# Decay attention, gated MLP and a top-1 mixture of experts on one core: the decay's bias by a matmul, swapped keys from the transpose

## The chip, the cores and the metric

The kernel runs on one NeuronCore of a Trainium2 chip. A core has a matrix engine (PE, with weight loads as PEld), a vector engine (DVE), a scalar engine (ACT), a general engine (POOL), and a queue engine (SP) that here issues nearly all transfers; 16 DMA engines move the data. Each engine runs its instructions in the order in which they were written to it. The metric is the device time of one execution in microseconds (us).

## The reference

Inputs: q, k, v of shape (4 batches, 8 heads, 576 positions, 64), forget gates f of shape (4, 8, 576), and the weights of two MLPs; output: 2304 x 512 in float32.

```python
scores = scale * np.matmul(q, k.transpose(0, 1, 3, 2))
log_f = np.log(np.clip(f, 0.0001, 1.0))
cum = np.cumsum(log_f, axis=-1)
decay = cum[:, :, :, None] - cum[:, :, None, :]
scores = np.where(causal, -1000000000.0, scores + decay)   # causal: key after query
...                                                        # softmax over keys
attn_out = np.matmul(attn, v)
x = attn_out as (2304, 512)
x = (silu(x @ w_gate) * (x @ w_val)) @ w_out               # d_ff 1536
...                                                        # x to one of 8 experts, 512 -> 1024 -> 512
```

In a softmax over keys the term cum[query] cancels, so only -cum[key] has to enter a row of scores. It is the same for all 576 query rows of a head.

## The kernel before

**Stages.** The program works on 32 heads, two heads (a pair P) at a time, 16 pairs, four pairs a batch. One head is two items: query blocks 0 to 2 (64, 128 and 128 rows; g = 0) and blocks 3 and 4 (128 rows each; g = 1), so 64 items. `slot(i)` (line 439) issues three things: `part1(i)`, the scores, row maxima and exponentials of item i; `part2(i-1)`, the split of the exponentials in two f16 parts and their DMA transpose; `pv(i-2)`, the product with the values. In the same slots the next pair is prepared: `scales`, `prep_v`, `prep(P+1, 0)`, `prep(P+1, 1)` and the loads of the pairs after it. The first 18 slots (batch 0) run while the gated MLP's weights, stored as 8-byte numbers, are loaded and decoded (`decode`, line 836). Then MLP units (`unit`, line 1067; 9 groups of 256 tokens with 6 units each, a unit being 24 + 24 matmuls of line 490 and 12 of line 543) are written between the remaining slots by a pacing table (`pts_`, line 1117): batch 1's slots within units 5 to 10, batch 2's within 11 to 23, batch 3's within 24 to 34. The units left and the experts follow without attention.

**Precision.** q and k are scaled by a power of two and split into f16 high and low parts; a head's `qks` tile holds, per 128-position chunk, 64 columns high and 64 columns low. One DMA transpose (line 210) turns it into `qkt` with dimensions on the partitions: high on 0 to 63, low on 64 to 127. A score is high x high + low x low (line 244, q and k with equal halves) plus high x low + low x high (line 246), for which the key's halves are swapped: `ksw`, made by two DVE copies (lines 214, 215) that wait for the transpose.

**The bias.** The cumulative sums `fz` (32 heads x 576) go to the DRAM tensor `cum_d` (line 757). For each head one row is loaded into all 128 partitions (`cb`, line 218, on SP), multiplied by the pair's scale on POOL (line 219), and subtracted by DVE's `tensor_tensor_reduce` (line 310), which also takes the row maximum. For batches 0 to 2 (`inner`) the causal mask is a third matmul (line 250); for batch 3 it is added to `cb` on POOL in place (line 290), and line 310 then runs in two pieces, one against `cb` and one against the masked tile.

**Order.** The program is not run as written line by line: a scheduler places each engine's instructions by its own estimate of when they could start, so an edit can also shift instructions that it doesn't name. Buffers are rings: two each of `qks` and `qkt`, five score tiles `s`, four of `p16`, three PSUM banks for scores.

**Other names.** `jk` (line 185) is scratch in the `qks` ring; `mx`, `nb`: row maxima and the bias of the exponential; `pt`: transposed probabilities; `xr`: attention output, transposed, the MLP's input; `raw`, `wg`, `wv`: raw weight buffers; `vr`: values read once more for a batch's scale; `id_d`, `g_d`: routing tables in DRAM, written once per 256 tokens, four bytes at a time.

## Time and profile before

| | |
|---|---|
| median of 3 runs | 1080.13 us (1072.58 to 1081.8) |
| profiled execution | 1090.63 us, its span 1088.5 us |
| mean granted TensorE clock | 0.917 of full |
| busy share of the span | PE 81%, DVE 62%, ACT 49%, POOL 42% |
| DMA | 149.55 MB, 259697 of 298584 packets under 512 B |
| scores start / end | 19.9 us / 609 us |

The profile gives, for one execution, each instruction's start and duration, and for idle time of an engine what ended it. Busy shares over the whole span mix stages with different limits, so they are read by stage: batch 0 with the weight loads, 0 to 175 us; MLP units alone, 175 to 225; batch 1 with its units, 225 to 295; batch 2, 295 to 470; batch 3, 470 to 612; MLP and experts without attention, from 612. A PE duration holds the whole latency of a matmul; back to back matmuls overlap, so their price is the distance between starts.

### The profile page before, as it was taken

Reading aid. Unit: us, or ns where it says so; the run is one execution under the profiler, and the core shown is the slowest. Engines: PE = TensorE matmul, PEld = TensorE weight load, DVE = VectorE, ACT = ScalarE, POOL = GpSimd, SP = SyncE. Lnnn points to the kernel's source line nnn. Section 1 sums busy time; section 2 is a strip of 40 time slices with the busy share of each in tenths; the row PEclk is TensorE's granted clock in tenths of the full one; section 3 lists DMA queues with packets and bytes.
Section 4 is the critical chain, followed back from the end, with each engine's and each line's share of the span. In section 5 each row is a group of like instructions: output and inputs, shape, how many; then the busy total and the mean of one; then the engine's idle time right before and its main releaser. Section 6 shows DMA issues by size and latency. Waiting matters only on the chain. (4 is left out here: it accounts for less than half of the span.)

```text
span 1088.5 us, 19531 instructions
## 1 busy us (share of the span) xinstructions
PE 880.6 (81%) x6789; PEld 726.5 (67%) x6789; DVE 677.0 (62%) x1946; ACT 537.0 (49%) x1160; POOL 458.3 (42%) x544
## 2 busy tenths in 40 slices
PE   1444448887976859899788899999877998999995
PEld 1333337765855648677667678888767887898994
DVE  4899799586675757777587542233334776665450
ACT  5877778464555636546264332222213645554441
POOL 2487676555344634466477412222215732110111
PEclk9995558998987979999989999999988999999998
DMA  8899889257778897767567360102328996555420
GB/s 222 186 228 221 189 171 216 63 121 158 166 102 155 144 127 155 148 108 147 84 103 155 45 194 11 40 1 39 59 48 207 255 218 190 167 181 164 173 100 31
DMA packets 298584, 149.55 MB, mean 137 GB/s; under 512 B 259697, under 2 KB 272113, under 8 KB 298484
## 3 DMA queue, kind: packets, MB, share of 16 engines
q1 hardware_dynamic: 294144, 137.83, 57.7%
q0 software_dynamic: 4096, 10.24, 3.9%
q8 instruction: 54, 0.88, 0.4%
q14 instruction: 46, 0.38, 0.2%
q10 hardware_dynamic: 244, 0.22, 0.1%
HBM read 91.06 MB, written 10.38 MB: 93 GB/s over the span
## 5 line engine op out<-in xcount | busy, mean ns | idle before, releaser
L490 PE MATMUL g<-xr,wg 128*128 128x256 f16 x1296 | 166.4, 282 | 18.9 <-ACT xr L433 10.5
L490 PE MATMUL v<-xr,wv 128*128 128x256 f16 x1296 | 170.1, 283 | 1.8 <-DVE t L523 1.2
L490 PEld LDWEIGHTS <-wv 128*128 128x128 f16 x1296 | 129.6, 103 | 32.9 <-issue 11.4
L490 PEld LDWEIGHTS <-wg 128*128 128x128 f16 x1296 | 125.1, 101 | 38.3 <-issue 16.9
L345 POOL TENSOR_TENSOR p<-st,p 128x128 f16<-128x128 f32 (+3 forms) x128 | 111.9, 880 | 45.1 <-DVE p L342 34.8
L530 POOL TENSOR_TENSOR lo<-t,hi 128x512 fp32r<-128x512 f32 x54 | 71.1, 1316 | 138.4 <-ACT hi L529 123.3
L380 PE MATMUL px<-vs,pt 128*128 128x64 f16 x1280 | 62.8, 207 | 65.1 <-DMA pt<-p 56.8
L380 PEld LDWEIGHTS <-pt 128*128 128x128 f16 x1280 | 55.6, 108 | 80.8 <-DMA pt<-p 64.2
L320 ACT ACTIVATE st<-st,nb,c 128x64 f32<-128x64 f32 (+4 forms) x160 | 102.7, 643 | 2.0
L342 DVE CAST p<-st 128x64 f16<-128x64 f32 (+4 forms) x160 | 74.4, 484 | 19.7 <-ACT st L320 16.2
L356 POOL TENSOR_TENSOR p<-st,p 128x64 f16<-128x64 f32 (+1 forms) x128 | 57.0, 448 | 54.0 <-issue 34.7
L529 ACT ACTIVATE hi<-t 128x512 fp32r<-128x512 f32 x54 | 33.7, 624 | 85.1 <-DVE t L523 85.1
L977 POOL DMA_INDIRECT out_dram<-o,ix x24 | 25.4, 1057 | 114.9 <-ACT o L1216 71.4
L244 PE MATMUL ps<-qkt 128*128 128x64 f16 (+3 forms) x192 | 54.6, 316 | 20.7 <-DVE mx L310 14.6
L1214 PE MATMUL bank<-whi,h 128*128 128x512 f32 x200 | 66.8, 399 | 3.7 <-ACT h L1176 2.9
L513 ACT ACTIVATE t<-g,gscale 128x512 f32<-128x512 f32 (+3 forms) x72 | 39.3, 570 | 60.2 <-PE g L490 60.1
L516 DVE SCALAR_TENSOR_TENSOR t<-t,g 128x512 f32<-128x512 f32 x54 | 36.8, 681 | 47.2 <-ACT t L513 45.4
L943 DVE TENSOR_TENSOR wlo<-wr,whi 128x1024 fp32r<-128x1024 f32 x48 | 57.6, 1244 | 13.7 <-ACT whi L942 12.9
L219 POOL TENSOR_TENSOR cb<-cb,c 128x576 f32<-128x576 f32 x32 | 38.5, 1204 | 61.2 <-DMA cb<-cum_d 53.5
L543 PE MATMUL yp<-wohi,hi 128*128 128x512 f32 x144 | 60.0, 417 | 0.0
L1171 PE MATMUL bank<-xh,whi 128*128 128x320 f32 (+1 forms) x192 | 59.4, 312 | 0.5 <-ACT xh L93 0.5
L246 PE MATMUL ps<-ksw,qkt 128*128 128x64 f16 (+2 forms) x192 | 56.5, 318 | 4.0 <-DVE ksw L215 3.9
(295 smaller groups left out, 2295.1 us busy)
## 6 DMA issues: line engine op xcount, KB each, us to landing
wr<-in_moe_w_dram SPq DMA_DIRECT2D x72, 512.0 KB, 5.0
cb<-cum_d SPq DMA_DIRECT2D x32, 288.0 KB, 4.3
vr<-in_v_dram SPq DMA_DIRECT2D x16, 288.0 KB, 4.9
qk_in<-in_q_dram SPq DMA_DIRECT2D x32, 128.0 KB, 2.7
qk_in<-in_k_dram SPq DMA_DIRECT2D x32, 128.0 KB, 3.0
v_in<-in_v_dram SPq DMA_DIRECT2D x32, 128.0 KB, 3.8
y_d<-ys SPq DMA_DIRECT2D x6, 512.0 KB, 3.4
wg<-in_moe_w_gate_dram SPq DMA_DIRECT2D x5, 512.0 KB, 4.4
```

Of the source, the lines that this page charges most:

```text
L246: pe.matmul(out=ps[:, o:o + n], lhsT=lq, rhs=ksw[:, k0 - 64:k1 - 64], start=False, stop=(d1 <= d0), skip_group_check=True)
L320: act.activation(out=sts[m], in_=sts[m], func=ACTF.Exp, scale=c[:, 0:1], bias=nb[:, m:m + 1], accum_out=sm[:, m, hh:hh + 1],)
L342: vec.tensor_copy(out=flat[:, o + 64:o + 64 + n], in_=src)
L345: gp.tensor_tensor(out=flat[:, o1:o1 + n - 64], in0=src[:, 64:n], in1=flat[:, o + 128:o + 64 + n], op=ALU.subtract)
L356: gp.tensor_tensor(out=blk[:, :, 0:64], in0=pair, in1=blk[:, :, 64:128], op=ALU.subtract)
L380: pe.matmul(out=px[:, 128 * m + 64 * hh:128 * m + 64 * hh + 64], lhsT=pm[:, o + ph * last + c, :], rhs=vs[:, hh, c, vh, :], start=(c == 0 ...
L490: pe.matmul(out=ps[:, fi, :], lhsT=w16[:, j, kk, wi, 128 * fi:128 * fi + 128], rhs=xr[:, kk, x0:x0 + 2, xi, :], start=(n_ == 0), stop=(n_ ...
L530: last["lo"] = gp.tensor_tensor(out=lo, in0=t, in1=hi.bitcast(F32), op=ALU.subtract)
L543: pe.matmul(out=yps[g][i], lhsT=hx[:, fi, 128 * i:128 * i + 128], rhs=wo[fk][wx], start=(j == 0 and n_ == 0), stop=(j == KF // 2 - 1 and n ...
L943: (eng or vec).tensor_tensor(out=l_, in0=t, in1=h_.bitcast(F32), op=ALU.subtract)
L1171: pe.matmul(out=p, lhsT=w[wi][:, kk, 128 * fk:128 * fk + 128], rhs=x[xi][:, kk, c0:CAP], start=(n_ == 0), stop=(n_ == 3 * KD - 1),)
L1214: pe.matmul(out=p[0:m, :], lhsT=hx, rhs=wx, start=(n_ == 0), stop=(n_ == len(prods) - 1))
```

## The change

`cum_d` and `cb` go. The cumulative sums are split once into three bf16 pieces that together hold them, and kept in SBUF as `cum3`: partitions 32 i to 32 i + 31 hold piece i of all 32 heads. A one-time table `pick` is -1 where the partition's head equals the column's head; per pair ACT scales it into `nc`, 128 columns for each head. A matmul with `nc` as weights and `cum3` as moving operand then adds -scale x cum[key] to every row of a score tile. The DVE step stays and subtracts a zero. The mask is a matmul for all four batches (`MB`, `inner`, `masked` and POOL's additions go). `qks` grows from 10 to 15 chunks of 128 columns: the second copy of the keys has its halves swapped, its high half written by the same ACT instruction as the first (output of 640 instead of 320 elements), its low half by one more ACT copy. The DMA transpose delivers the swapped keys in `qkt[:, 2]`, and the two DVE copies go.

```diff
@@ consts @@
+        pick_i = c_p.tile([128, B * H], I32, tag="c", name="pick_i")
+        gp.iota(pick_i, [[-1, B * H]], base=0, channel_multiplier=1)
+        vec.tensor_single_scalar(out=pick_i, in_=pick_i, scalar=B * H - 1, op=ALU.bitwise_and)
+        vec.tensor_scalar(out=pick, in0=pick_i, scalar1=0.0, scalar2=-1.0, op0=ALU.is_equal, op1=ALU.mult)
+        vec.memset(cum3, 0.0)
+        vec.memset(zero, 0.0)
@@ scales @@
+        nc_ = st_p.tile([128, 2, 128], BF16, tag="nc", bufs=2, name="nc")
+        h0 = P // NP * H + 2 * (P % NP)
+        act.activation(
+            out=nc_, in_=pick[:, h0:h0 + 2].rearrange("p (h o) -> p h o", o=1).to_broadcast([128, 2, 128]),
+            func=ACTF.Copy, scale=c[:, 1:2],
+        )
@@ prep @@
-        qks = qks_p.tile([128, 2, NCH, 2, D], F16, tag="qks", name="qks")
-        for a in range(2):
+        qks = qks_p.tile([128, 3 * NCH, 2, D], F16, tag="qks", name="qks")
...
+        for a, n in ((0, 1), (1, 2)):
...
-            act.activation(out=hi, in_=src, func=ACTF.Copy, scale=s1)
+            act.activation(
+                out=part(w, w + D, 2) if n > 1 else hi, func=ACTF.Copy, scale=s1,
+                in_=src.rearrange("p (o c) d -> p o c d", o=1).to_broadcast([128, 2, NCH, D]) if n > 1 else src,
+            )
             vec.scalar_tensor_tensor(out=lo, in0=src, scalar=s1, in1=hi, op0=ALU.mult, op1=ALU.subtract)
...
-        ksw = qkt_p.tile([128, S], F16, tag="ksw", name="ksw")
-        vec.tensor_copy(out=ksw[0:64, :], in_=qkt[64:128, 1, 64:])
-        vec.tensor_copy(out=ksw[64:128, :], in_=qkt[0:64, 1, 64:])
-        cb = cb_p.tile([128, S], F32, tag="cb", name="cb")
-        b, h = P // NP, 2 * (P % NP) + hh
-        sp.dma_start(out=cb, in_=cum_d[b * H + h:b * H + h + 1, :].to_broadcast([128, S]))
-        gp.tensor_tensor(out=cb, in0=cb, in1=c[:, 1:2].to_broadcast([128, S]), op=ALU.mult)
-        heads[P, hh] = (qkt, ksw, cb)
+        act.activation(out=qks[:, 2 * NCH:, 0, :], in_=lo, func=ACTF.Copy)
+        qkt = qkt_p.tile([128, 3, NCH * 128], F16, tag="qkt", name="qkt")
+        sp.dma_start_transpose(out=qkt.rearrange("p a (c t) -> p (a c) t", t=128), in_=flat)
+        heads[P, hh] = (qkt, c[1][:, hh, :])
@@ score @@
-        d0, d1 = max(k0, 128 * j), k1 if inner else max(k0, 128 * j)
+        pe.matmul(out=ps[:, o:o + n], lhsT=lq, rhs=qkt[:, 2, k0:k1], start=False, stop=False, skip_group_check=True)
+        d0 = max(k0, 128 * j)
         pe.matmul(
-            out=ps[:, o:o + n], lhsT=lq, rhs=ksw[:, k0 - 64:k1 - 64], start=False, stop=(d1 <= d0), skip_group_check=True
+            out=ps[:, o:o + n], lhsT=pk, rhs=cum3[:, k0 - 64:k1 - 64], start=False, stop=(k1 <= d0),
+            skip_group_check=True,
         )
@@ part1 @@
-        if not inner:
-            for m in range(nt):
...
-                gp.tensor_tensor(
-                    out=sts[m][:, k0 - 64:k1 - 64], in0=cb[:, k0 - 64:k1 - 64], in1=masked[:, k0 - k1 + 128:], op=ALU.add
-                )
...
-                d0 = k1 if inner else min(max(k0, 128 * j), k1)
-                for a, b, bias in ((k0, d0, cb), (d0, k1, sts[m])):
...
+                vec.tensor_tensor_reduce(
+                    out=sts[m][:, k0 - 64:k1 - 64], in0=ps[:, o:o + n], in1=zero.to_broadcast([128, n]),
+                    scale=1.0, scalar=init, op0=ALU.subtract, op1=ALU.max, accum_out=mx[:, x:x + 1],
+                )
@@ start @@
-        act.dma_start(out=cum_d, in_=fz)
+        for i in range(3):
+            hi = c_p.tile([128, S], BF16, tag="c", name="cumhi")[0:B * H]
+            vec.tensor_copy(out=hi, in_=fz)
+            vec.tensor_copy(out=cum3[B * H * i:B * H * i + B * H, :], in_=fz)
+            if i < 2:
+                vec.tensor_tensor(out=fz, in0=fz, in1=hi, op=ALU.subtract)
```

The scheduler moves more than these lines. On SP, at the start of the program, before the change (`wg_91`: a raw weight buffer; `vr`: the values of batch 0; `qkt<-qks`: head 0's transpose):

```order
L826 DMA raw<-in_moe_w_gate_dram 128x4x256
L826 DMA wg_91<-in_moe_w_gate_dram 128x4x256
L794 DMA vr<-in_v_dram 128x576 x4
L210 DMA_TRANSPOSE qkt<-qks 128x10x128
L218 DMA cb<-cum_d 128x576
```

and with the change:

```order
L832 DMA raw<-in_moe_w_gate_dram 128x4x256
L832 DMA wg_92<-in_moe_w_gate_dram 128x4x256
L800 DMA vr<-in_v_dram 128x576 x4
L832 DMA wv_93<-in_moe_w_val_dram 128x4x256
L832 DMA wg_92<-in_moe_w_val_dram 128x4x256
L832 DMA wv_93<-in_moe_w_out_dram 128x1024
L170 DMA qk_in_98<-in_k_dram 128x4x64
L170 DMA qk_in_99<-in_q_dram 128x4x64
L168 DMA qk_in_98<-in_k_dram 64x2x64
L170 DMA qk_in_98<-in_k_dram 128x4x64
L168 DMA qk_in_99<-in_q_dram 64x2x64
L231 DMA_TRANSPOSE qkt<-qks 128x15x128 x2
```

Three weight loads of 512 KB and five pieces of the next pairs' q and k now stand ahead of the first two heads' transposes, which are issued together. On DVE, where the first 256 tokens are routed in the midst of batch 1 (`rb`, `eq`: routing; `t`, `xs`: MLP and attention output; lines 310 and 311 are the reduction on scores), before:

```order
L689 TENSOR_TENSOR rb<-eq,tokm 128x2x24
L713 TENSOR_TENSOR rb<-eq,gw 128x2x24
L214 COPY ksw<-qkt 64x576
L215 COPY ksw<-qkt 64x576
L342 CAST p_0_101<-st 128x448
L310 ISA st,mx<-ps,cb 128x64
L310 ISA mx 128x1
L310 ISA st,mx<-ps,cb 128x192
```

and with the change:

```order
L690 TENSOR_TENSOR rb<-eq,tokm 128x2x24
L714 TENSOR_TENSOR rb<-eq,gw 128x2x24
L517 SCALAR_TENSOR_TENSOR t<-t,g 128x512
L807 TENSOR_SCALAR gscale<-sw,sv 128x6
L410 TENSOR_TENSOR xs<-xn,xs 128x3x128
L808 SCALAR_TENSOR_TENSOR hscale<-sw,sv,gscale 128x6
L311 ISA st,mx<-ps,zero,mx 128x512
L311 ISA mx 128x1
L717 TENSOR_TENSOR ixf<-ixf,rk 128x48
L311 ISA st,mx<-ps,zero 128x64
```

Behind the routing steps stood the two copies that wait for a transpose, with the casts and reductions of other items behind them; now nothing on DVE at this place waits for a transpose of keys.

## Rows read from the trace of the kernel before

**Rows 1.** Busy time by stage: us, busy (xinstructions) per engine, granted clock, DMA share, GB/s.
```profile
0.00:175.00 175.00, 74.08 (x588) 52.92 (x589) 145.33 (x406) 129.22 (x312) 111.77 (x124) 0.78 0.90 205
225.00:295.00 70.00, 59.85 (x568) 47.86 (x568) 51.45 (x144) 41.14 (x105) 36.93 (x48) 0.93 0.71 147
295.00:470.00 175.00, 140.83 (x1356) 112.67 (x1355) 120.72 (x432) 90.84 (x240) 81.61 (x109) 0.88 0.82 139
470.00:612.00 142.00, 124.49 (x1183) 99.28 (x1181) 106.06 (x396) 68.87 (x177) 85.54 (x132) 0.96 0.64 114
```

**Rows 2.** PE's waits, 225 to 612 us: us in total, times, longest.
```profile
PE px L380 <- DMA pt<-p: 35.4, 18, 11.0
PE ps L244 <- DVE mx L310: 11.0, 8, 4.6
```

**Rows 3.** Waits of DVE and POOL, 225 to 612 us.
```profile
DVE ksw L214 <- DMA qkt<-qks: 37.7, 10, 9.8
...
POOL cb L219 <- DMA cb<-cum_d: 39.8, 11, 6.8
```

**Rows 4.** Timeline of DVE: start, us, instruction, [idle before <-releaser].
```profile
309.30 0.30 DVE L214 COPY ksw<-qkt 64x576 f16<-64x576 f16 x1 [6.58 <-DMA qkt<-qks]
...
402.21 1.46 DVE L214 COPY ksw<-qkt 64x576 f16<-64x576 f16 x1 [9.76 <-DMA qkt<-qks]
...
545.26 0.30 DVE L214 COPY ksw<-qkt 64x576 f16<-64x576 f16 x1 [6.55 <-DMA qkt<-qks]
```

**Rows 5.** Timeline of PE, its stops near these places.
```profile
226.00 0.19 PE L246 MATMUL ps<-ksw,qkt 128*128 128x64 f16 x1 [2.21 <-DVE ksw L215]
...
310.92 0.56 PE L770 MATMUL tot<-am,onesf 128*128 128x2 f32 x2 [6.01 <-DVE mx L310]
...
401.29 0.55 PE L380 MATMUL px<-vs,pt 128*128 128x64 f16 x7 [11.03 <-DMA pt<-p]
...
480.55 4.45 PE L490 MATMUL g<-xr,wg 128*128 128x256 f16 x24 [2.43 <-DVE t L516]
...
546.26 0.61 PE L244 MATMUL ps<-qkt 128*128 128x512 f16 x1 [4.62 <-DVE mx L310]
```

**Rows 6.** The clock after such a stop: columns as in rows 1.
```profile
314.00:316.00 2.00, 2.00 (x7) 1.61 (x6) 1.97 (x6) 0.51 (x3) 1.97 (x5) 0.50 0.10 17
```

**Rows 7.** Chain of waits, late MLP: start, us, 24 matmuls of one unit.
```profile
689.41 2.64 PE g L490 x24
```

**Rows 8.** Groups of instructions, 0 to 620 us: busy, mean ns, idle before.
```profile
L214 DVE COPY ksw<-qkt 64x576 f16<-64x576 f16 x32 | 18.5, 580 | 44.7 <-DMA qkt<-qks 44.1
...
L215 DVE COPY ksw<-qkt 64x576 f16<-64x576 f16 x32 | 12.7, 396 | 0.5
...
L219 POOL TENSOR_TENSOR cb<-cb,c 128x576 f32<-128x576 f32 x32 | 38.5, 1204 | 61.2 <-DMA cb<-cum_d 53.5 <-PE ps L246 4.5 <-DVE ys L574 2.5
...
L310 DVE CUSTOM_DVE_ANT_0 st<-ps,cb 128x64 f32<-128x64 f32 x56 | 12.1, 216 | 4.8 <-POOL cb L219 3.9 <-PE ps L250 0.7
...
L290 POOL TENSOR_TENSOR st<-cb,masked 128x128 f32<-128x128 f32 x32 | 14.3, 472 | 0.0
```

**Rows 9.** Timeline of PE: score matmuls back to back; distances of starts.
```profile
494.08 0.35 PE L244 MATMUL ps<-qkt 128*128 128x448 f16 x1
494.27 0.35 PE L246 MATMUL ps<-ksw,qkt 128*128 128x448 f16 x1
494.46 0.19 PE L244 MATMUL ps<-qkt 128*128 128x64 f16 x1
```

**Rows 10.** ACT groups that price the new ACT work.
```profile
L207 ACT ACTIVATE qks<-qk_in,sc 128x320 f16<-128x320 f32 x64 | 30.8, 549 | 8.4 <-DVE sc L780 8.4
...
L185 ACT ACTIVATE jk<-qk_in 128x640 f16<-128x640 f32 x32 | 23.3, 729 | 39.6 <-DMA qk_in<-in_k_dram 21.9 <-DMA qkt<-qks 15.6 <-DVE fz L756 1.8
```

**Rows 11.** Two us each: one lone 8-chunk transpose (262 KB); plain weight loads.
```profile
706.00:708.00 2.00, 2.00 (x21) 1.79 (x19) 0.00 (x0) 0.00 (x0) 1.19 (x1) 1.00 0.71 131
632.00:634.00 2.00, 2.00 (x21) 1.80 (x19) 0.69 (x1) 0.69 (x1) 0.00 (x0) 1.00 0.94 354
```

More of the change, by code (lines that the diff above doesn't have):

```diff
@@ L21 @@
 MASKED = -float(2 ** 100)
-MB = 3
 EXP1 = 1 << 23
@@ L84 @@
     rg = const.tile([128, KD, 32], F32, name="rg")
+    cum3 = const.tile([128, S], BF16, name="cum3")
+    pick = const.tile([128, B * H], F32, name="pick")
+    zero = const.tile([128, 1], F32, name="zero")
     sel = const.tile([128, NE], F32, name="sel")
@@ L201, in prep, with part @@
         sc, c = stt[P]
-        qks = qks_p.tile([128, 2, NCH, 2, D], F16, tag="qks", name="qks")
-        for a in range(2):
+        qks = qks_p.tile([128, 3 * NCH, 2, D], F16, tag="qks", name="qks")
+        flat = qks.rearrange("p c h d -> p (c h d)")
+        w = 2 * NCH * D
+        def part(o, step, n):
+            dims = [list(flat.ap[0])] + ([[step, n]] if n > 1 else []) + [[2 * D, NCH], [1, D]]
+            return type(flat)(flat.tensor, flat.offset + o, dims)
+        for a, n in ((0, 1), (1, 2)):
             src = qk_in[(2 * P + a) % NQK][:, hh]
             s1 = sc[:, 0, a:a + 1]
-            hi, lo = qks[:, a, :, 0, :], qks[:, a, :, 1, :]
-            act.activation(out=hi, in_=src, func=ACTF.Copy, scale=s1)
-            vec.scalar_tensor_tensor(out=lo, in0=src, scalar=s1, in1=hi, op0=ALU.mult, op1=ALU.subtract)
-        qkt = qkt_p.tile([128, 2, NCH * 128], F16, tag="qkt", name="qkt")
-        sp.dma_start_transpose(
-            out=qkt.rearrange("p a (c t) -> p (a c) t", t=128), in_=qks.rearrange("p a c h d -> p (a c h d)")
-        )
-        ksw = qkt_p.tile([128, S], F16, tag="ksw", name="ksw")
-        vec.tensor_copy(out=ksw[0:64, :], in_=qkt[64:128, 1, 64:])
-        vec.tensor_copy(out=ksw[64:128, :], in_=qkt[0:64, 1, 64:])
-        cb = cb_p.tile([128, S], F32, tag="cb", name="cb")
-        b, h = P // NP, 2 * (P % NP) + hh
-        sp.dma_start(out=cb, in_=cum_d[b * H + h:b * H + h + 1, :].to_broadcast([128, S]))
-        gp.tensor_tensor(out=cb, in0=cb, in1=c[:, 1:2].to_broadcast([128, S]), op=ALU.mult)
-        heads[P, hh] = (qkt, ksw, cb)
+            hi, lo = [qks[:, NCH * a:NCH * a + NCH, x, :] for x in range(2)]
+            act.activation(
+                out=part(w, w + D, 2) if n > 1 else hi, func=ACTF.Copy, scale=s1,
+                in_=src.rearrange("p (o c) d -> p o c d", o=1).to_broadcast([128, 2, NCH, D]) if n > 1 else src,
+            )
+            vec.scalar_tensor_tensor(out=lo, in0=src, scalar=s1, in1=hi, op0=ALU.mult, op1=ALU.subtract)
+        act.activation(out=qks[:, 2 * NCH:, 0, :], in_=lo, func=ACTF.Copy)
+        qkt = qkt_p.tile([128, 3, NCH * 128], F16, tag="qkt", name="qkt")
+        sp.dma_start_transpose(out=qkt.rearrange("p a (c t) -> p (a c) t", t=128), in_=flat)
+        heads[P, hh] = (qkt, c[1][:, hh, :])
     vsp = {}
@@ L238, with score @@
     sums = {}
-    def score(ps, o, hd, j, k0, k1, inner):
-        qkt, ksw, _ = hd
+    def score(ps, o, hd, j, k0, k1):
+        qkt, pk = hd
         n = k1 - k0
@@ L296, in part1 @@
             for j, k0, k1 in grp:
-                score(ps, o, hd, j, k0, k1, inner)
+                score(ps, o, hd, j, k0, k1)
                 o += k1 - k0
@@ L303, in part1 @@
                 init = seen.get(m, -3e38)
-                d0 = k1 if inner else min(max(k0, 128 * j), k1)
-                for a, b, bias in ((k0, d0, cb), (d0, k1, sts[m])):
-                    if a < b:
-                        left[m] -= b - a
-                        x = m if not left[m] else nx
-                        nx += left[m] > 0
-                        vec.tensor_tensor_reduce(
-                            out=sts[m][:, a - 64:b - 64], in0=ps[:, o + a - k0:o + b - k0], in1=bias[:, a - 64:b - 64],
-                            scale=1.0, scalar=init, op0=ALU.subtract, op1=ALU.max, accum_out=mx[:, x:x + 1],
-                        )
-                        init = seen[m] = mx[:, x:x + 1]
+                left[m] -= n
+                x = m if not left[m] else nx
+                nx += left[m] > 0
+                vec.tensor_tensor_reduce(
+                    out=sts[m][:, k0 - 64:k1 - 64], in0=ps[:, o:o + n], in1=zero.to_broadcast([128, n]),
+                    scale=1.0, scalar=init, op0=ALU.subtract, op1=ALU.max, accum_out=mx[:, x:x + 1],
+                )
+                seen[m] = mx[:, x:x + 1]
                 o += n
```

19 lines of the change are left out of this document (5 added, 14 removed).

## The prediction

> **What bounds the kernel now.** I read the windows by stage first [rows 1]. In the first stage (0 to 175 us, batch 0 beside the weight loads) PE is busy 74 of 175 us; DMA has a share of 0.90 and DVE is busy 145.33 us (0.83), ACT 129 (0.74), POOL 112 (0.64): transfers and DVE limit it together, PE does not. In the three stages after it PE is busy 59.85 of 70, 140.83 of 175 and 124.49 of 142 us, so it is idle for 10, 34 and 17.5 us, and DVE, ACT and POOL have more room than PE. From 612 us on the change touches nothing. So: work taken from DVE, POOL and DMA is worth something before 175 us; work given to PE costs something between 225 and 612 us, unless it lands in PE's idle time. What that idle time is decides the case.
>
> The list of waits says what ends it [rows 2]: 35.4 us for transposed probabilities and 11.0 us for row maxima from DVE. Row maxima are late because DVE is held: it stood 37.7 us for the keys' transpose, in ten stops, at its first swap copy, with casts and reductions of other items behind it; POOL stood 39.8 us for `cb` [rows 3]. The timelines set the two side by side. DVE waits 6.58 us at 309.30 and PE stops 6.01 us for a maximum up to 310.92; DVE 6.55 us at 545.26 and PE 4.62 us up to 546.26. At 226.00 PE waits 2.21 us for a swap copy itself, and 2.43 us up to 480.55 for another late DVE result [rows 4, 5]. A stop costs more than its length: after the one at 310.92 the granted clock is still 0.50, the 1.2 GHz level, from 314 to 316 us [rows 6], and after the one at 480.55 the next 24 matmuls took 4.45 us [rows 5], where they take 2.64 at full clock [rows 7]. The longest stop is another kind: DVE waits 9.76 us up to 402.21, but PE's 11.03 us up to 401.29 are for a transpose of probabilities that lands as late as the keys' one [rows 4, 5]. There the transfers are late, and no engine's order matters.
>
> **The change, part by part**, against the profiled execution (1090.63 us; its span is 1088.5). That execution is 10.5 us above the median of the runs, 1080.13; I carry the differences over to the median unchanged.
>
> *Swap copies go (DVE).* 0.580 + 0.396 us a head [rows 8], 0.98 us. The first 18 slots prepare pairs 0 to 4, ten heads, before 175 us: 9.8 us. DVE's share there is 0.83, so -8 us. The other 22 heads free 21.5 us of DVE.
>
> *`cb` goes (POOL, SP, DMA).* 1.204 us a head on POOL [rows 8]: 26.5 us for 22 heads, and in batch 3 also the mask additions, 14.3 us, together 41 of POOL's 204 us between 225 and 612 [rows 1], 20%. In batch 3 DVE's reductions run in 6 pieces a head instead of 10, with the same columns: 32 pieces fewer, at no more than the 0.216 us of the smallest shape [rows 8], 6.9 us. A wait for maxima or probabilities that is left on PE ends behind casts, reductions and subtractions on these two engines. Of 46 us [rows 2] and the 6 us at 310.92 some 40 us remain after the next term; I let them shrink by POOL's 20%: -8 us. Ends: 0, if they are DMA's alone, and -20, by half.
>
> *The stops at the swap copy.* The four PE stops named above sum to 6.01 + 4.62 + 2.43 + 2.21 = 15.3 us. DVE no longer stands there; what is late next is PE's own score matmul on `qkt`, which the written order puts behind MLP matmuls, or the probabilities' transpose. I take -12 us; ends 0 and -15.3. With each stop goes the slow stretch behind it, 4.45 - 2.64 = 1.8 us; four stops' 7.2 us in the same proportion are -6 us; ends 0 and -7.2.
>
> *The bias matmul and batch 3's masks (PE).* Back to back, 448 columns take 494.27 - 494.08 = 0.19 us [rows 9]. A head has 1600 score columns, at that rate 0.68 us; 22 heads 14.9 us. The masks add 576 columns for 8 heads: 2.0 us. Batch 1's stage is dense, so its 8 heads' 5.4 us count in full; of the other 11.5 us I count half, as PE is idle there for 52 us in 32 slots, 1.6 us a slot. +11.2 us; ends +4 and +16.9. The swapped keys' matmul is no addition: it replaces the one on `ksw`.
>
> *ACT.* The key's high half with 640 outputs instead of 320: 0.729 - 0.549 = 0.18 us; the copy of the low half as a 320-element row, 0.549; half a pair's `nc`, at most 0.27 [rows 10]: 1.0 us a head, 22 us between 225 and 612, where ACT is busy 201 of 387 [rows 1]. The copy waits for DVE's low half, and exponentials may stand behind it. ACT is off the bound but on the chain from maxima to probabilities: a fifth, +4 us; ends 0 and +22.
>
> *The transpose.* A lone transpose of 8 chunks, 262 KB, moved 131 GB/s at a DMA share of 0.71 [rows 11], 184 GB/s of busy time; five more chunks, 164 KB, cost 0.89 us of all DMA engines. `cb`, 295 KB, at the plain loads' 354 GB/s in a share of 0.94 [rows 11] cost 0.78 us. So DMA gains nothing: 0 us. The Trainium skill (Advanced Engine Details and Errata, X-Bar Transpose) has transposes on trn2 as fast as ordinary transfers; by it the five chunks would cost half of that, and I estimate another -3 us in the first stage. The rows speak against it.
>
> *The start.* Three loads of 512 KB and 0.45 MB of q and k now stand ahead of the first transposes on SP, 2.0 MB; at the first stage's 205 GB/s [rows 1] attention starts up to 9.8 us later. The same bytes are then missing from later queues, so it is worth 0 to 9.8; I take +4. The split of the sums, eight small DVE steps, falls where DVE has no other work.
>
> *Sum:* -8 + 4 before 175 us; +11.2 - 12 - 6 - 8 + 4 after 225 us: -14.8 us. **1080.1 - 15 = 1065 us.** The terms are of both signs and of one size, so only their balance is forecast.
>
> **Rivals.**
> 1. *PE becomes the bound, slower.* Place: 295 to 612 us. If its 52 us of idle time there are set by late transfers, as at 401.29, they stay and move behind the added matmuls: 16.9 us in full, and neither DVE's nor POOL's lighter load buys anything. For it: the longest stop is of this kind, and 35.4 of the waits are for a DMA. Against it: four stops that are DVE's own. 1080 + 17 = 1097. It decides if PE's idle time from 225 to 612 us stays at 62 us or above. Chance 0.22.
> 2. *The wait only changes its owner, flat.* The change wouldn't remove the stop but hand it on: PE itself stands for a transpose that is longer and comes after one more ACT step. The -12 and -6 fall away: -4 + 11.2 - 8 + 4 = +3, 1083. For it: the transposes are queued on SP behind the same probabilities. Against it: scores are placed well behind their head's preparation. Chance 0.26.
> 3. *DVE and POOL were the limit.* DVE's full 9.8 us before 175 us with no late start, the stops with their slow stretches in full, the other waits halved: -9.8 + 11.2 - 15.3 - 7.2 - 20 + 4 = -37, 1043. For it: 78 us of head-of-line stops [rows 3]. Against it: DMA's share of 0.90 before 175 us. Chance 0.10.
>
> The forecast has 0.42; with its terms half-way to their ends it reaches from some 1052 to 1080.
>
> **How the numbers follow.** A measurement of this kernel can't tell a change of under 1%, 10.8 us, from none; that bound lies at 1069. Faster by more: 0.30 of the forecast, rival 3's 0.10 and 0.03 of rival 2, 0.43. Within 1%: 0.12 of the forecast, 0.19 of rival 2 and 0.04 of rival 1, 0.35. Slower: 0.18 of rival 1 and 0.04 of rival 2, 0.22. The range takes in rival 1 and nearly rival 3: 1045 to 1098.
>
> **What would show it.** Right: DVE and POOL have no stop for a transfer of keys or `cb`; scores on PE run at the distances of [rows 9] with one matmul more; PE's waits for maxima between 225 and 612 us fall from 17 us to under 6; PE's idle time there falls although its work grows by 17 us; the first score matmul comes up to 10 us after 19.9 us, while the first MLP matmuls keep their place. Wrong: PE waiting for `qkt` by 10 us or more in sum, the waits for probabilities above 35 us, or ACT waiting at the new copy with exponentials behind it.

## The result, and the profile after

The changed kernel takes **1034.7 us** in the median (1031.1 to 1036.55 in 4 runs) against 1080.91 (1072.58 to 1081.8) for the kernel before in the same runs: a ratio of 0.9585, 95% interval 0.953 to 0.964. The forecast was 1065, its range 1045 to 1098: the direction is right, the gain of 46 us is three times the forecast, and the time lies below the range. The profiled execution took 1036.55 us, its span is 1034.8 us (before 1088.5).

The page of the changed kernel, busy time of each engine and share of the span:

```profile
PE 885.4 (86%) x7003; PEld 738.0 (71%) x7029; DVE 632.2 (61%) x1829; ACT 558.0 (54%) x1208; POOL 397.6 (38%) x473
```

Its windows at the same places of the program as [rows 1] (columns as there):

```profile
0.00:168.00 168.00, 80.42 (x660) 58.53 (x666) 144.71 (x416) 140.56 (x342) 98.08 (x117) 0.76 0.90 215
211.00:281.00 70.00, 61.28 (x611) 49.35 (x613) 50.63 (x169) 46.10 (x118) 34.37 (x46) 0.98 0.74 151
281.00:438.00 157.00, 138.72 (x1357) 112.37 (x1363) 100.78 (x356) 96.50 (x250) 65.59 (x96) 0.95 0.70 141
438.00:573.00 135.00, 131.40 (x1313) 108.04 (x1320) 86.89 (x331) 74.29 (x187) 59.84 (x84) 0.99 0.60 112
```

The stretch of MLP units ahead of batch 1 (not among the rows) fell from 50 to 43 us; batch 1's stage kept its length, batch 2's fell from 175 to 157 us and batch 3's from 142 to 135. In the three stages of the batches PE is idle for 8.7, 18.3 and 3.6 us, where it was idle for 10, 34 and 17.5. PE's waits between 211 and 573 us (us in total, times, longest), the answer to [rows 2]:

```profile
PE px L381 <- DMA pt<-p: 9.6, 10, 1.8
...
PE ps L256 <- DVE mx L311: 2.4, 2, 1.8
...
PE ps L256 <- DMA qkt<-qks: 1.7, 1, 1.7
```

Waits for transposed probabilities fell from 35.4 to 9.6 us, those for maxima from 11.0 to 2.4, and the new transpose of 15 chunks holds PE for 1.7 us. The stops of [rows 3] have no successor: the waits of DVE and POOL name no transfer of keys and no `cb`. PE's timeline (first the first score of all) has the scores at the distances of [rows 9], 0.19 us for 448 columns, with the bias matmul (L259) and the mask (L264) behind them:

```profile
27.01 0.23 PE L256 MATMUL ps<-qkt 128*128 128x64 f16 x1 [3.94 <-DMA qkt<-qks]
...
440.11 0.35 PE L256 MATMUL ps<-qkt 128*128 128x448 f16 x1
440.30 0.35 PE L257 MATMUL ps<-qkt 128*128 128x448 f16 x1
440.49 0.35 PE L259 MATMUL ps<-cum,nc 128*128 128x448 bf16 x1
440.68 0.22 PE L264 MATMUL ps<-maskgt,negid 128*128 128x128 bf16 x1
```

ACT's groups with the new work, to be set beside [rows 10]:

```profile
L224 ACT ACTIVATE qks<-qk_in,sc 128x640 f16<-128x640 f32 x32 | 26.1, 814 | 0.0
...
L229 ACT ACTIVATE qks<-qks 128x320 f16<-128x320 f16 x32 | 14.3, 458 | 8.4 <-DVE qks L228 8.4
...
L202 ACT ACTIVATE nc<-pick,c 128x256 bf16<-128x256 f32 x16 | 7.9, 492 | 0.0
```

They cost what was forecast from [rows 10], and the first score comes at 27.01 us, 7.1 later than before.

**A clock for comparing.** I read the start of DVE's first step of each MLP unit (line 516 before, 517 after): the same places of the program in every kernel. Unit 0 ends the first stage, batch 3's slots end with unit 35, and unit 53 is the last before the experts. Before, unit 0 stands at 174.1, unit 35 at 633.2, unit 53 at 791.2 us; after, at 167.9, 588.5 and 745.5. So 6.2 us come from the first stage, **38.5 us from units 0 to 35**, 1.0 from 35 to 53, and 8.0 from the end, code that the change doesn't touch. The profiled execution of before, 1090.63 us, is longer than every other execution of that kernel on record (1069.68 to 1088.12), so these differences are rather too large. The windows from unit 0 to unit 35, before and then after:

```profile
174.10:633.20 459.10, 387.12 (x3598) 310.70 (x3598) 318.68 (x1060) 237.86 (x600) 236.16 (x316) 0.93 0.69 128
```

```profile
167.90:588.50 420.60, 388.28 (x3740) 317.07 (x3759) 273.94 (x931) 246.99 (x616) 188.40 (x252) 0.97 0.63 128
```

The transfers of SP's queue in these windows, before and then after: packets, MB, share of the 16 engines' time (100% would be all 16 busy throughout):

```profile
q1 hardware_dynamic: 174195, 58.19, 68.0%
```

```profile
q1 hardware_dynamic: 184172, 53.31, 62.2%
```

PE's busy time is the same, 387.1 and 388.3 us, though it has the bias and mask matmuls on top: the granted clock rose from 0.93 to 0.97. Its idle time fell from 72.0 to 32.3 us. And the transfers took 68.0% of 459.1 = 312 us of the 16 engines' time before, 62.2% of 420.6 = 262 us after, 50 us less; the forecast had put no change there.

### The profile page after: what moved, and what is told of

It reads as the page before. It is cut to its first block, busy times and chain, and to the rows that moved or that the text cites. A ratio compares the mean times of both kernels' runs of the same rounds, so it can differ in the third digit from the quotient of the medians.

```text
span 1034.8 us, 19815 instructions
## 1 busy us (share of the span) xinstructions
PE 885.4 (86%) x7003; PEld 738.0 (71%) x7029; DVE 632.2 (61%) x1829; ACT 558.0 (54%) x1208; POOL 397.6 (38%) x473
## 3 DMA queue, kind: packets, MB, share of 16 engines
q1 hardware_dynamic: 310016, 133.63, 55.7%
## 4 chain that ended last, share of the span: by engine, by line
PE 42%; DMA 7%; issue 6%; ACT 3%; DVE 2%; POOL 2%; SPq 1%; POOLq 0%; DVEq 0%; ACTq 0%
PE bank L1220 9%; PE bank L1177 8%; PE yp L544 8%; PE v L491 7%; PE g L491 6%; DMA pair<-yt 1%; DMA out_dram<-o,ix 1%; POOL xg L1051 1%; PE px L381 1%; DMA qkt<-qks 1%; DMA pt<-p 1%; DMA pair<-words 1%; ACT st L321 1%; DMA wr<-in_moe_w_dram 1%; DVE st L311 1%
## 5 line engine op out<-in xcount | busy, mean ns | idle before, releaser
L491 PE MATMUL v<-xr,wv 128*128 128x256 f16 x1296 | 162.4, 281 | 0.0
L491 PE MATMUL g<-xr,wg 128*128 128x256 f16 x1296 | 161.4, 278 | 0.5 <-DMA xr<-xs 0.5
L346 POOL TENSOR_TENSOR p<-st,p 128x128 f16<-128x128 f32 (+3 forms) x128 | 108.7, 854 | 79.1 <-issue 52.4
L381 PE MATMUL px<-vs,pt 128*128 128x64 f16 x1280 | 58.7, 203 | 41.0 <-DMA pt<-p 30.0
L343 DVE CAST p<-st 128x64 f16<-128x64 f32 (+4 forms) x160 | 71.8, 464 | 30.7 <-ACT st L321 21.9
L381 PEld LDWEIGHTS <-pt 128*128 128x128 f16 x1280 | 52.4, 106 | 52.4 <-DMA pt<-p 35.1
L256 PE MATMUL ps<-qkt 128*128 128x64 f16 (+2 forms) x192 | 56.7, 311 | 25.9 <-DMA qkt<-qks 11.3
L357 POOL TENSOR_TENSOR p<-st,p 128x64 f16<-128x64 f32 (+1 forms) x128 | 54.2, 425 | 61.5 <-DVE p L343 30.6
L311 DVE CUSTOM_DVE_ANT_0 st<-ps,zero 128x64 f32<-128x64 f32 (+3 forms) x160 | 55.6, 376 | 24.2 <-PE ps L264 21.0
L257 PE MATMUL ps<-qkt 128*128 128x64 f16 (+2 forms) x192 | 59.9, 315 | 0.0
```

The costliest lines, as they stand in the source:

```text
L257: pe.matmul(out=ps[:, o:o + n], lhsT=lq, rhs=qkt[:, 2, k0:k1], start=False, stop=False, skip_group_check=True)
L311: vec.tensor_tensor_reduce(out=sts[m][:, k0 - 64:k1 - 64], in0=ps[:, o:o + n], in1=zero.to_broadcast([128, n]), scale=1.0, scalar=init, op ...
L343: vec.tensor_copy(out=flat[:, o + 64:o + 64 + n], in_=src)
L346: gp.tensor_tensor(out=flat[:, o1:o1 + n - 64], in0=src[:, 64:n], in1=flat[:, o + 128:o + 64 + n], op=ALU.subtract)
L381: pe.matmul(out=px[:, 128 * m + 64 * hh:128 * m + 64 * hh + 64], lhsT=pm[:, o + ph * last + c, :], rhs=vs[:, hh, c, vh, :], start=(c == 0 ...
L491: pe.matmul(out=ps[:, fi, :], lhsT=w16[:, j, kk, wi, 128 * fi:128 * fi + 128], rhs=xr[:, kk, x0:x0 + 2, xi, :], start=(n_ == 0), stop=(n_ ...
```

## The experiments

Theory A: the stops of DVE at the swap copies and of POOL at `cb` cost the time. Theory B: the work taken from DVE and POOL. Theory C: an order of the transfers; theory D, added later: the load of `cb`'s row itself. All runs at a glance; the ratios are to the kernel before in the same runs (its median there 1076.7 to 1081.3 us); "bytes" is the part of `cb`'s row that is loaded, "busy" and "transfers" are PE's and those of SP's queue (16 engines' time) from unit 0 to 35:

| run | time, us | ratio to before (95%) | unit 0 at | units 0 to 35 | bytes | busy | transfers |
|---|---|---|---|---|---|---|---|
| before | 1080.9 | 1 | 174.1 | 459.1 | 1 | 387.1 | 312 |
| after | 1034.7 | 0.9585 (0.953 to 0.964) | 167.9 | 420.6 | 0 | 388.3 | 262 |
| e1_masks | 1075.5 | 0.9997 (0.997 to 1.003) | 175.1 | 444.7 | 1 | 382.9 | 306 |
| e3_bias | 1055.6 | 0.9808 (0.975 to 0.987) | 182.8 | 421.5 | 0 | 386.7 | 247 |
| e4_pe | 1065.6 | 0.9889 (0.985 to 0.993) | 177.1 | 435.8 | 0 | 400.2 | 277 |
| e5_dvewait | 1035.0 | 0.9630 (0.957 to 0.969) | 167.8 | 421.0 | 0 | 391.3 | 265 |
| e6_dvework | 1081.5 | 1.0026 (1.000 to 1.006) | 215.4 | 419.6 | 0 | 386.5 | 271 |
| e7_poolwait | 1056.6 | 0.9837 (0.977 to 0.990) | 176.2 | 432.1 | 1/3 | 393.6 | 274 |
| e8_poolwork | 1034.5 | 0.9621 (0.956 to 0.968) | 167.8 | 419.7 | 0 | 388.9 | 263 |
| e9_nocb | | | 176.3 | 423.7 | 0 | 376.2 | 245 |
| e10_loadonly | | | 169.5 | 446.9 | 1 | 383.5 | 296 |
| e11_loadmul | | | 178.9 | 443.6 | 1 | 388.8 | 289 |
| e12_nomul | | | 168.9 | 453.4 | 1 | 385.5 | 315 |
| e13_casts | 1050.9 | 0.9737 (0.969 to 0.979) | 181.9 | 420.2 | 0 | 386.2 | 265 |
| e14_load3 | 1054.5 | 0.9794 (0.974 to 0.985) | 172.4 | 431.6 | 1/3 | 391.9 | 285 |
| e15_load4c | 1050.1 | 0.9754 (0.973 to 0.978) | 183.9 | 418.3 | 1/144 | 386.0 | 259 |
| e16_loadact | 1062.9 | 0.9868 (0.984 to 0.989) | 188.5 | 429.2 | 1/3 | 390.8 | |
| e17_maskdve | 1052.5 | 0.9790 (0.975 to 0.983) | 172.2 | 424.0 | 0 | 385.4 | 301 |
| e18_maskdve2 | 1038.4 | 0.9630 (0.960 to 0.966) | 171.1 | 417.1 | 0 | 382.6 | 282 |
| e19_pad32 | 1041.8 | 0.9652 (0.962 to 0.969) | 167.2 | 427.4 | 0 | 389.4 | 287 |

Runs e9 to e12 compute other values, the bias being left out or unscaled; what follows unit 35 (routing and experts) takes longer in them, 1204 to 1229 us in all, so their totals say nothing on the expectations, and I compare them up to unit 35.

**One part alone (e1, e3).** e1 is the kernel before with `MB = 4`:

```diff
-MB = 3
+MB = 4
```

> The kernel before with the masks of batch 3 entered by the matmul, as in the other three batches; POOL loses its 40 mask additions there and TensorE gains as many short matmuls. Theory A (the stops of DVE and POOL behind their loads are what the change took away): 1080 us, within 5, since every stop stays. Theory B (the work taken from DVE and POOL is what counts): about 1070 us, nearly all of it won between units 24 and 35 of the projections. Theory C (an order of the transfers is what counts): no change.

No difference in the time; its trace, of an execution of 1071.65 us, serves as a second one of before: 444.7 us from unit 0 to 35 instead of 459.1. So 24 to 38 us of the gain are to be explained there. e3 is the changed kernel with the keys swapped by copies again:

```diff
-        qks = qks_p.tile([128, 3 * NCH, 2, D], F16, tag="qks", name="qks")
+        qks = qks_p.tile([128, 2, NCH, 2, D], F16, tag="qks", name="qks")
...
+        vec.tensor_copy(out=ksw[0:64, :], in_=qkt[64:128, 1, 64:])
+        vec.tensor_copy(out=ksw[64:128, :], in_=qkt[0:64, 1, 64:])
```

> The changed kernel, but the swapped keys are again made by two DVE copies that wait for the keys' transpose; the bias and the masks stay in the matmul. Theory A: the stops of DVE at the copies come back, and with them about half of the gain or more, 1055 to 1065 us. Theory B: DVE gets back 31 us of copies but ScalarE and the transpose lose their added work, and POOL stays relieved, so about 1048 us. If POOL's stop at the row of cumulative sums was the one that mattered: 1040 us or less.

The total, 1055.6, would fit theory A, but the stages don't: from unit 0 to 35 it takes 421.5 us, like the changed kernel, although DVE stands there for the keys' transposes longer than in the kernel before ([rows 3]: 37.7 us in 10 stops):

```profile
DVE ksw L224 <- DMA qkt<-qks: 43.4, 18, 6.1
```

It is not the stops alone that come back: e3 also lacks ACT's added work and a third of each keys' transpose, so its equal time is a balance. The 15 us that it loses lie before unit 0. There the scheduler's order differs: 85 of the first 220 rows of SP have no match in the changed kernel's order.

**The wait or the work alone, on DVE and POOL (e5, e6, e7, e8).** After the head's preparation in the changed kernel, one of (buffers' declarations and the write of `cum_d` are left out here and below):

```diff
+        vec.tensor_copy(out=tst[:, 0:1], in_=qkt[:, 1, 64:65])                                   # e5
+        for x in (0, 64, 0):                                                                     # e6
+            vec.tensor_copy(out=jw[x:x + 64, :], in_=cum3[64 - x:128 - x, 0:384])
+        sp.dma_start(out=cb, in_=cum_d[..., 0:S // 3].to_broadcast([128, S // 3]))               # e7
+        gp.tensor_tensor(out=cb[:, 0:1], in0=cb[:, 0:1], in1=c[0][:, 1:2], op=ALU.mult)
+        for _ in range(3):                                                                       # e8
+            gp.tensor_tensor(out=jb, in0=jb, in1=c[0][:, 1:2].to_broadcast([128, 192]), op=ALU.mult)
```

> The changed kernel with one DVE copy of a single column per head, written where the two swap copies stood, that waits for the transpose of the head's keys: the wait of before without its work. Theory A: the stops of DVE come back, and the time rises by about 20 us to 1055 us, with DVE waiting 30 to 40 us for the transposes. Theory B: one short instruction per head, 32 of them, adds 1 to 3 us: 1036 to 1038 us.

The wait is there and costs nothing. DVE stands at the added copy for 26.1 us in 13 stops from unit 0 on; the waits row and two of its stops in the timeline of e5:

```profile
DVE tst L233 <- DMA qkt<-qks: 26.1, 13, 4.9
```

```profile
265.82 0.16 DVE L233 COPY tst<-qkt 128x1 f16<-128x1 f16 x1 [3.68 <-DMA qkt<-qks]
...
370.85 0.16 DVE L233 COPY tst<-qkt 128x1 f16<-128x1 f16 x1 [4.88 <-DMA qkt<-qks]
```

The order of PE and SP is that of the changed kernel row by row, so this is the wait alone: 0.4 us. In this order theory A falls for DVE. At single places of the kernel before it does not: the maxima that ended PE's stops of 6.01 and 4.62 us [rows 5] run right behind the swap copies for which DVE had stood [rows 4]:

```profile
310.26 0.22 DVE L310 CUSTOM_DVE_ANT_0 st<-ps,cb 128x64 f32<-128x64 f32 x1
...
545.91 0.28 DVE L310 CUSTOM_DVE_ANT_0 st<-ps,st,mx 128x64 f32<-128x64 f32 x1
```

> The changed kernel with three POOL multiplies of 128 x 192 per head on a buffer of zeros, where the multiply of the cumulative sums stood: its work (1.2 us a head in one piece, some 40 to 50 us in three) without its wait. Theory A: within 5 us of the changed kernel, up to 1040 us. Theory B: 1045 us or more.

POOL's work comes back (226.8 us busy from unit 0 to 35 instead of 188.4) and costs nothing either.

> The changed kernel with three DVE copies of 64 x 384 bf16 per head of a constant, where the two swap copies stood: their work without their wait, some 0.3 us each, 28 us in all. Theory A (stops): within 5 us of the changed kernel, 1035 to 1040 us. Theory B (work): 10 us or more slower, 1045 to 1055 us.

This missed its aim. The copies wait for nothing, so the scheduler put all 96 ahead of their heads, before 102 us, where DVE is scarce:

```profile
23.54 4.66 DVE L234 COPY jw<-cum 64x384 bf16<-64x384 bf16 x13
```

Unit 0 comes at 215.4 us, 47.5 later for 36 us of copies, and from there on it runs as the changed kernel does. It shows that DVE's work, or the order that it forces, is dear in the first stage; for the stage after, it says nothing on work in its place.

> The changed kernel with the cumulative sums written to memory again, a load of 192 of their columns to all partitions per head from SP's queue, and a POOL multiply of one column that waits for it: the wait of before, and a third of its transfer, without its work on POOL. Theory A: POOL's stops come back and hold up what is queued behind them (the differences that go into the weights' transposes): 1045 to 1055 us. Theory B: 1036 to 1040 us.

22 us slower than the changed kernel, 11.5 of them between units 0 and 35: the first run in which that stage moved without more matmuls. It has both the wait and a third of the load.

**The row's path taken apart, on the kernel before (e9 to e12).** Theory D is the load itself, E POOL's stop, F the chain from the load to the maxima. e9 reads zeros instead of the row and neither loads nor scales it; e10 loads it for nobody; e11 loads and scales it for nobody; e12 loads it and lets DVE read it unscaled (shortened; where e9 to e11 leave the row out, POOL's mask additions read zeros too):

```diff
-        sp.dma_start(out=cb, in_=cum_d[b * H + h:b * H + h + 1, :].to_broadcast([128, S]))       # e9
-        gp.tensor_tensor(out=cb, in0=cb, in1=c[:, 1:2].to_broadcast([128, S]), op=ALU.mult)      # e9, e10, e12
+        vec.tensor_copy(out=cb[:, 0:1], in_=c[:, 1:2])      # e10, e12: ahead of the load
-    in1=bias[:, a - 64:b - 64]                              # e9, e10, e11
+    in1=zero.to_broadcast([128, b - a])
```

> The kernel before without the bias: the row of cumulative sums is neither loaded nor scaled and the maxima read zeros in its place (the bias is left out of the scores); swap copies, masks and TensorE's work as before. Theory D, E and F all say that the row's path (load, POOL multiply, DVE) is what costs after the first stage, so 1035 to 1045 us; if the swap copies matter after the first stage as well, 1060 us or more.

> As the last, but each head's row is loaded, into a buffer that nobody reads (one DVE copy of a single column ahead of the load keeps it at its head). Theory D (the load's own traffic and its place in SP's queue): within 8 us of the kernel before, 1070 to 1078 us. Theory E (POOL stopped behind the load) and F (the maxima wait for the load by way of POOL): within 5 us of the run without the row.

> The kernel before with the row loaded and scaled by POOL as before, but the maxima read zeros (bias left out of the scores). Theory D or E: within 8 us of the kernel before. Theory F: as the run without the row.

> The kernel before with the row loaded and read by the maxima directly, without POOL's scaling (the bias enters unscaled). Theory E: POOL no longer stops, so within 8 us of the run without the row. Theory D or F: within 8 us of the kernel before, 1070 to 1078 us.

Without the row 423.7 us, with the swap copies and their stops still there (30.0 us of DVE's waits). With the load that nobody reads 446.9, 23.2 more, as much as with the scaling (443.6) and within the kernel before's own 444.7 to 459.1. D holds; E and F add nothing that stands out. 8.1 of the 23.2 us are one place: PE waits there for a routing step, 12.4 us instead of 4.3. No packet of a row is under way in the 19 us before the end of the longer wait, so this part is not shown to be the load's. In e9 the routing step stands behind a swap copy that waits, so one stop of DVE does reach PE without the load:

```profile
378.77 0.31 DVE L216 COPY ksw<-qkt 64x576 f16<-64x576 f16 x1 [6.60 <-DMA qkt<-qks]
...
379.79 1.09 PE L693 MATMUL rk<-rb,ra 128*128 128x48 f32 x4 [4.34 <-DVE rb L713]
```

The windows from unit 0 to 35 of e9 and then of e10 show the load on the clock:

```profile
176.30:600.00 423.70, 376.17 (x3568) 302.91 (x3567) 287.50 (x1034) 226.99 (x574) 199.16 (x286) 0.97 0.59 118
```

```profile
169.50:616.40 446.90, 383.49 (x3604) 310.74 (x3600) 302.57 (x1078) 237.06 (x597) 210.07 (x295) 0.94 0.67 130
```

The same matmuls take 376.2 us of PE at a clock of 0.97 and 383.5 at 0.94. How a load for nobody can stop PE is to be seen in e10 at 541 us, in SP's queue and on PE:

```profile
541.82 0.53 SPq L221 DMA_DIRECT2D cb<-cum_d  x1
542.51 1.29 SPq L361 DMA_TRANSPOSE pt<-p  x1
543.90 0.53 SPq L221 DMA_DIRECT2D cb<-cum_d  x1
544.61 1.63 SPq L361 DMA_TRANSPOSE pt<-p  x1
```

```profile
543.80 0.93 PE L492 MATMUL g<-xr,wg 128*128 128x256 f16 x7
547.13 0.58 PE L382 MATMUL px<-vs,pt 128*128 128x64 f16 x14 [2.40 <-DMA pt<-p]
```

A load is issued ahead of each of two transposes of probabilities, and PE stands 2.40 us for a transpose. The trace's packets show the two kinds side by side. The transposes move in packets of 256 bytes: of those that start from 542.0 to 542.5 us, with no packet of the row among them, each takes 18 ns in the mean; from 544.25 to 544.75, with 17 packets of the row (2304 bytes each) started among them, 81 ns. PE's stops of over 2.5 us from 168 to 633 us: 8 with 39.2 us in the kernel before, 3 with 9.6 after, 3 with 10.1 in e9, 5 with 28.4 in e10.

**Bytes or queue (e14, e15, e16).** The changed kernel with 192 columns, with 4, or with 192 from ACT's queue, read by nobody:

```diff
+        vec.tensor_copy(out=cb[:, 0:1], in_=c[0][:, 1:2])
+        sp.dma_start(out=cb, in_=cum_d[..., 0:S // 3].to_broadcast([128, S // 3]))               # e14
+        sp.dma_start(out=cb[:, 0:4], in_=cum_d[..., 0:4].to_broadcast([128, 4]))                 # e15
+        act.dma_start(out=cb, in_=cum_d[..., 0:S // 3].to_broadcast([128, S // 3]))              # e16
```

> The changed kernel with a third of the row (192 of 576 columns, 96 KB to 128 partitions) loaded per head from SP's queue into a buffer that nobody reads; POOL does not wait for it. If the load itself costs, as the run with the unread row says: 10 us more between units 0 and 35 (430 instead of 420) and 1045 to 1055 us in all. If POOL's stop made the 22 us of the run with the POOL wait: 1035 to 1040 us.

> The same with 4 of the 576 columns (16 bytes to each partition): the same issues and waits in SP's queue, 1/48 of the bytes. If bytes cost: 1035 to 1038 us and 420 to 422 us between units 0 and 35. If the place in the queue costs: as the run with 192 columns.

> The run with 192 columns, its load issued from ScalarE's queue instead of SP's. If bytes cost: 430 us between units 0 and 35, as from SP's queue. If SP's queue is what the load holds up: 420 to 422 us there, unless ScalarE itself is held.

From unit 0 to 35: 431.6, 418.3, 429.2. The bytes cost, the place in the queue doesn't: the same number of packets with 16 bytes each is free, and ACT's queue helps little. Over all runs, one execution of each, this stage sorts by bytes alone, whatever else was edited: 417 to 427 us in the eleven kernels without the row or with four columns of it (e4, with its added matmuls, left aside), 429 to 432 in the three with a third, 444 to 459 in the five with the whole. POOL's wait in e7 (50.2 us in 11 stops for the load; 432.1) adds nothing to the load without it (431.6). (Four columns are 1/144 of the row; the text on record counts 1/48, of the 192 columns.) The totals miss the expectations of e15 and e16 by the first stage, below.

**PE or the transfers (e4, e17, e18, e19).** e4 adds a matmul with weights of zeros to each score segment; e17 and e18 take the mask matmuls away and let DVE subtract a constant row of zeros and mask, e18 with the buffers in another place; e19 puts 32 unused bytes ahead of the attention's buffers:

```diff
+            pe.matmul(out=ps[:, o:o + n], lhsT=zw, rhs=cum3[:, k0 - 64:k1 - 64], start=False, ...)   # e4
-                out=ps[:, o + d0 - k0:o + k1 - k0], lhsT=negid, rhs=maskgt[...]                      # e17, e18
+                in1=mz[:, z0:z0 + n],                                                                # e17, e18
+    pad = ap_.tile([128, 8], F32, name="pad")                                                        # e19
```

> The changed kernel with one more matmul per segment of a score, of a weight of zeros and the width of the segment, so that TensorE has some 22 us more to do and no other engine anything. If TensorE is now what sets the pace after the first stage: 1050 us. If the gain came from an engine that still sets the pace beside it (DVE or the transfers): 1040 us or less. Above 1057 us would mean that the added matmuls delay the maxima as well as fill TensorE.

> The changed kernel without the matmuls that enter the masks: the maxima subtract, instead of a zero, a constant row of zeros and mask of their segment's width, so DVE and POOL have no more to do and TensorE 192 short matmuls less, some 14 us, 9 of them between units 0 and 35. If TensorE ends that stage: 1022 to 1028 us, 411 us between units 0 and 35. If something else does beside it: 1032 us or more.

> The changed kernel without the mask matmuls, the masks in the constant row that the maxima subtract, and the attention's buffers moved by 256 bytes only. If TensorE ends the stage: 409 to 413 us between units 0 and 35, and SP's transfers 570 to 580 us of the 16 engines' time. If the transfers end it: 418 to 424 us there. The whole: 1024 us with a first stage of 168 us, up to 1040 us with one of 184 us.

> The changed kernel with 32 bytes of unused memory ahead of the attention's buffers. If the place of the buffers makes the transfers slow: SP's transfers take about 615 us of the 16 engines' time instead of 576, and 424 to 430 us between units 0 and 35. If not: 576 us and 420 us, and the time of the changed kernel but for its first stage.

Added matmuls count about in full: PE 11.9 us busier in e4, the stage 15.2 longer, with 16 us more of transfers. The whole, 1065.6, lies above 1057, from where on the text on record has the maxima delayed; PE's waits for them hardly grew (3.7 us in this stage, 2.4 in the changed kernel), and 9.2 us come before unit 0. Removed ones don't: in e17 PE is 2.9 us less busy and the stage 3.4 longer, in e18 5.7 less and 3.5 shorter. But in both the same bytes took 20 to 40 us more of the transfer engines. e19 shows that alone, by the place of the buffers: every engine has the changed kernel's order row by row (POOL one memset more), and the page's row on SP's queue, after and e19, reads

```profile
q1 hardware_dynamic: 310016, 133.63, 55.7%
```

```profile
q1 hardware_dynamic: 310016, 133.63, 58.7%
```

the same packets and bytes in 576 us of the engines' time (55.7% of 1034.8) and in 610 (58.7% of 1039.7). By size, all of it is in the packets of 256 bytes (transposes and pieces of q, k and v): 356.5 us in the changed kernel, 391.5 in e19, all others 219.3 and 218.5. The stage is 6.8 us longer. e17 and e18, with one order on SP and two places of the buffers, are a second such pair: 619 and 588 us over the whole, 424.0 and 417.1 in the stage. So after the change PE and the transfers bound it together. The sum of the engines' time is not the price by itself, though: e17's transfers take as much of it between units 0 and 35 as e10's, 301 and 296 us, in a stage 23 us shorter. No run beat the changed kernel; e5 and e8 equal it.

**The first stage.** Unit 0 stands at 167.2 to 167.9 us in the changed kernel and in the three runs whose order is its own or nearly so (e5, e8, e19). Where the scheduler shifted more (67 to 126 of SP's first 220 rows without a match, e6 and the runs on the kernel before left aside), it stands at 171 to 188, whatever the edit: 183.9 with four columns to load (e15), 181.9 with 8 us of casts taken from DVE (e13):

```diff
-                vec.tensor_copy(out=flat[:, o + 64:o + 64 + n], in_=src)
+                (gp if P < 6 and n < 320 else vec).tensor_copy(out=flat[:, o + 64:o + 64 + n], in_=src)
```

> The changed kernel with the casts of 64 and 192 columns of the weights on POOL instead of DVE, for the first six pairs of heads: DVE loses 24 casts of 0.32 to 0.34 us, 8 us in the first stage, and POOL gets some 15 us. If DVE sets the first stage, as the run with added DVE copies says (36 us more there, 47 us later at unit 0): 1025 to 1030 us. If POOL's later weights hold the transposes up instead: 1035 us or more.

The relief was to give 4 to 10 us and unit 0 came 14 us later. The time goes with the order there, and the changed kernel's is the best seen; what in the order costs was not tried. Of the totals of e3, e13, e15 and e16, 14 to 21 us are this.

## Why the prediction was wrong

**The step that failed** is *The transpose*: "`cb`, 295 KB, at the plain loads' 354 GB/s in a share of 0.94 cost 0.78 us. So DMA gains nothing: 0 us." The load was priced by another kind of load [rows 11], and as if it cost only its own packets. e1 and e3 have the same transposes and differ in SP's queue by the loads:

```profile
q1 hardware_dynamic: 294144, 137.83, 57.9%
```

```profile
q1 hardware_dynamic: 289536, 128.39, 52.4%
```

57.9% of 1069.9 = 619.5 us of the engines' time against 52.4% of 1054.1 = 552.3, 67 us for 32 loads, **2.1 us a load**. A third of it (e14 against e15: 599.5 and 576.5) is 0.72 us, in proportion. e10 and e9 give less, 53.8% of 1214.6 against 50.1% of 1200.3, 52 us, 1.6 a load. By packet size, the row's own packets take 1.05 us a load in e10 and 1.26 in the kernel before; the rest is that other transfers' packets get longer: the 243200 packets of 256 bytes take 331.6 us in e9 and 349.1 in e10. In e1 they take 362.6, and as e19 shows that the place of the buffers alone can add 35 us to them, a part of the 2.1 us may be the buffers' place, and so may a part of the gain; no run moved the buffers of the kernel before and nothing else. The other half of the step was right: five more chunks cost 576.4 - 552.3 = 24.1 us for 32 heads, 0.75 us, forecast 0.89. So a head gains some 0.9 to 1.35 us of all transfer engines where I had 0.11 lost, and the loads are worth 15 us (e9 and e10 without the routing step) to 23 us between units 0 and 35, from two fifths to nearly all of the 24 to 38 us gained there.

The rest of the gain stays open, and it need not be small. e9, without the row but with the swap copies and POOL's masks, has 12.1 us less PE work than the changed kernel and yet takes 3.1 us longer, where e4's 11.9 us of PE cost 15.2. So other parts of the change may be worth some 15 us in that stage beside the load; which of them, no run tells.

The Trainium skill (DMA: Bandwidth & Descriptors, Specifications) gives 512 bytes as the least transfer for line rate. The row's packets have 2304, and at 1.05 to 1.26 us a load they moved 234 to 281 GB/s of busy time where the weight loads moved 377 (354 at a share of 0.94), so here that size was not enough. Whether it matters that 128 partitions read the same row was not tried.

The other steps:
- *Stops at the swap copy, -12.* Not found as a term: 0.4 us for the stops alone (e5), and 421.5 against 420.6 us with the copies back (e3, which also saves transfers and ACT work). Two pairs of the timelines [rows 4, 5] were read rightly: PE's 6.01 and 4.62 us ended with maxima behind a copy, and in e9 4.34 us ended with a routing step behind one. But such a stop needs a late transpose first, and once the load is gone even 43.4 us of DVE's stops (e3) leave the stage as short as the changed kernel's. Which share of the gain runs through them is open.
- *Slow stretches, -6.* The mechanism was right, its owner wrong: the same matmuls take 387.1 us before (382.9 in e1, with batch 3's masks on top) and 376.2 in e9, up to 10.9 less, but with the load gone and the swap copies still there; with the load back 383.5.
- *Other waits by lighter POOL and DVE, -8.* Waits for probabilities from unit 0 to 35 fell from 38.7 to 11.2 us, but not by POOL's multiply: with as much work back (e8) nothing changed, and batch 3's masks alone (e1) gave nothing in the time. With the load gone and the rest as before (e9) they are 19.2 us. DVE's lighter work was not tried alone in this stage.
- *Bias matmul and masks, +11.2.* The work was forecast at 14.9 + 2.0 = 16.9 us and is smaller: 388.3 against 376.2 us at the same clock (e9), 12.1. From before to after it is paid out of PE's idle time and the clock; once the load is gone, matmuls count about in full (e4).
- *ACT, +4.* ACT's copy waits 8.4 us for DVE's low half in all, but e3, without the new ACT work, takes as long as the changed kernel: no cost seen.
- *First stage, -8 and +4.* Scores start 7.1 us later, as forecast up to 9.8; unit 0 comes 6.2 earlier. The size fits, but runs without a reason differ by 20 us there, so this is no evidence for either term.

Rival 3 came nearest, 1043, not for its reason: it let the stops of DVE and POOL and their lighter work pay, and putting one of them back into the changed kernel cost nothing (DVE's stops in e5, POOL's work in e8, POOL's stop in e7 against e14); its nearness is no evidence for it. Rival 1's mechanism, PE as the bound, is true only now that the load is gone (e4). No rival named the load. Of the signs listed, those for "right" nearly all came, and so could not tell the forecast's reasons from the true one: late transfers show in DVE's, POOL's and PE's waits alike.

## What to carry to other kernels

An engine that waits for a transfer is no proof that its wait costs: put the wait back alone and see. Price a load by its own kind, in engine time (share of the queue's row times the span), and with what it adds to the packets of the transfers beside it, before saying that bytes given and bytes taken cancel. Before taking such a price from two kernels, make sure that their buffers lie in the same place. And where a scheduler sets the order, compare stage by stage and look at whether the order moved: here one short copy and a load of four columns a head (e15) went with a first stage 16 us longer.
